# Linear attention and gated feed-forward, four layers: PSUM as four two-bank pairs, and attention scheduled by tiles

## The chip, the cores and the metric

The kernel runs on one core of a Trainium2 chip. The kernel before has a median of 1495.12 us.

TensorE is written PE (its weight loads PEld), VectorE DVE, ScalarE ACT, GpSimd POOL and SyncE SP, as in the profile.

## The reference, cut to what matters

```python
def _A_ref(x, wqkv, wo):               # x: 2048 x 1024, 32 heads of 32
    q, k, v = ...                       # x @ wqkv, by heads
    phi = lambda t: jnp.where(t > 0, t + 1, jnp.exp(t)) + 1e-6
    pq, pk = phi(q), phi(k)
    kv  = jnp.einsum("bhsd,bhse->bhde", pk, v)
    z   = jnp.einsum("bhsd->bhd", pk)
    num = jnp.einsum("bhqd,bhde->bhqe", pq, kv)
    den = jnp.einsum("bhqd,bhd->bhq", pq, z)[..., None] + 1e-6
    return (num / den) ... @ wo

def _B_ref(x, w_gate, w_up, w_down):    # hidden width 3584
    return ((x @ w_gate) * (x @ w_up)) @ w_down

x = A_x
x = x + _A_ref(_layernorm(x), A_wqkv, A_wo)
x = x + _B_ref(_layernorm(x), B_w_gate, B_w_up, B_w_down)
x = x + _A_ref(_layernorm(x), A_wqkv, A_wo)
x = x + _B_ref(_layernorm(x), B_w_gate, B_w_up, B_w_down)
```

The kernel calls the first and third lines "layer A" (attention) and the other two "layer B" (feed-forward). The same weights serve both layers of a kind. In a feed-forward layer the kernel forms seven products of half blocks, numbered 1 to 7, with sums in between, in place of eight; they run in the order 1, 2, 6, 5, 7, 3, 4.

## The kernel before: the parts that matter

PSUM is eight tiles of one bank each (128 x 512 float32). A "drain" below is an instruction of ACT or DVE that reads such a bank. `mm_tile` hands the banks out in turn.

```python
Q = [psum.tile([P, NB], F32, tag=f"Q{i}", name=f"Q{i}")[:] for i in range(8)]   # NB = 512

def phi(ps, dst, split=False):              # 512 columns
    e = turn("e", eb)
    # ... the split form takes a second ACT read (Identity) in place of DVE's read of PSUM
    nc.scalar.activation(out=e, in_=ps, func=ACT.Exp)
    nc.vector.tensor_scalar(out=e, in0=e, scalar1=1.0, scalar2=1e-6, op0=ALU.min, op1=ALU.add)
    nc.vector.scalar_tensor_tensor(out=dst, in0=ps, scalar=1.0 + 1e-6, in1=e, op0=ALU.add, op1=ALU.max)

def flush():                                # one pending action of a division
    if later:
        later.pop(0)()

def over_den(t):                            # division of one query tile: two actions
    # ...
    return [lambda: den_sums(pq, den), lambda: den_divide(t, pq, den)]
    # den_divide ends with the DMA transpose of the tile
```

While layer A runs for the first time, ACT also scans the weights of the feed-forward layers: a sum of squares of each of 42 blocks of 128 x 2048 (14 of gate, 14 of up, 14 of down). A scan needs its block in a buffer, and the end of a scan starts the fetch of a further block. The partial sums give a power-of-two scale per matrix: `scale_sum` on DVE, then one small matmul and a power in `scale_pow`.

```python
def scan_step(n=1):
    for _ in range(n):
        i = scanned[0]
        m, c = divmod(i, NU)                # NU = 14
        nc.scalar.activation(out=scan_buf[i], in_=scan_buf[i], func=ACT.Square, accum_out=acc[:, m, c:c + 1])
        scanned[0] += 1
        # ...
        scan_fetch()                        # DMA of a further block, issued from ACT's queue

def scale_sum(lo, hi):
    nc.vector.tensor_reduce(out=part[:, lo:hi], in_=acc[:, lo:hi, :], axis=AX.X, op=ALU.add)
    nc.vector.tensor_copy(out=partb[:, lo:hi], in_=part[:, lo:hi])

def scale_pow(lo, hi):
    ps = mm_tile()
    nc.tensor.matmul(out=ps[:, lo:hi], lhsT=ones[:], rhs=partb[:, lo:hi], start=True, stop=True)
    # ... max, power on POOL, bit mask
```

Layer A after the keys: query tiles, then kvo (the masked key-value product times the output weights), then output tiles, which also carry the last scans and the down scale:

```python
for t in range(XT_):                        # XT_ = 10
    q[2 * t]()
    scans()
    do(rest[...])                           # products xk, one bank each
    # ... t == 7: scale_sum(0, 2); t == 8: scale_pow(0, 2)
    q[2 * t + 1]()
    if t < 8:
        scans()
# ...
if first_A:
    # scale_sum(2, 3) in job 10, scale_pow(2, 3) in job 15
    for i in range(2, 9):                   # seven scans among the output tiles
        jobs[i] = [scans] + jobs.get(i, [])
```

Feed-forward: after products 1, 6 and 7 ACT copies the accumulator (a "snapshot"), as two copies of 512 columns; `vsum` on DVE adds two such halves to it later. The order of a unit, with the preparation of the next weights (`pr`) and of the down weights (`mine`, 2 us on ACT each, first layer only):

```python
elif p in (6, 7):
    snaps[u, p] = turn("sn", SN)
    for m in range(2):
        nc.scalar.copy(out=snaps[u, p][:, m, :], in_=a[m])
# ...
for u in range(NU):
    # ...
    gate_step(u, 1); gate_step(u - 1, 4)
    do(pr[0:2])
    gate_step(u, 2)
    pr[2]()
    gate_step(u - 1, 3); gate_step(u, 6)
    for x in mine: x[1]()                   # the down-weight scaling on ACT
    pr[3]()
    gate_step(u, 5); gate_step(u, 7)
    # ...
```

## Time and profile before

| | before |
|---|---|
| median of 3 runs | 1495.12 us (1494.37 to 1495.13) |
| span and granted clock of the profiled run | 1493.1 us, 1.00 |
| PE, DVE, ACT busy | 1477.1 (99%), 1060.9 (71%), 734.7 us (49%) |
| 364 matmuls of 512 columns in a row | 78.56 us, 215.8 ns each |

From the first part of the page of the kernel before, busy time of each engine in us, its share of the span, and the count of instructions:

```profile
PE 1477.1 (99%) x6895; PEld 675.9 (45%) x6997; DVE 1060.9 (71%) x1829; ACT 734.7 (49%) x914; POOL 66.4 (4%) x179
```

PE is the bound: 99% of the span at full clock. What can be won is the time in which PE starts no matmul. I read that in two ways: the view of waits, and the distances between starts of successive matmuls, in excess of 216 ns. The waits of PE in the kernel before (what PE waited for by line of the instruction and of its releaser: total, times, longest):

```profile
PE Q L528 <- ACT W L550: 1.1, 1, 1.1
...
PE Q L341 <- DMA XT<-ST: 0.9, 1, 0.9
PE Q L356 <- DVE K L331: 0.7, 1, 0.7
```

They are a few events of about 1 us each. L528 (products of the feed-forward layers) waits for a snapshot once; L341 (projections) for a DMA transpose once; L356 (xk) for phi once. In distances of starts these are 1.23, 1.10 and 0.88 us. (A missing record shows as a distance of twice 216 ns, and such distances are not counted as waits.)

The groups of instructions that the change widens, by shape (after the count: busy us, mean ns of one, then idle before and its releasers):

```profile
L218 ACT ACTIVATE K<-K 128x2048 bf16<-128x2048 bf16 x37 | 70.6, 1909 | 1.3 <-ACT K L218 0.9 <-DMA K<-in_B_w_down_dram 0.4
L550 ACT COPY MX<-Q 128x512 f32<-128x512 f32 x120 | 69.2, 585 | 96.4 <-PE Q L528 96.4
```

```profile
L493 DVE TENSOR_TENSOR W<-MX,Q 128x512 f16<-128x512 f32 x176 | 116.6, 684 | 28.7 <-ACT MX L550 16.5 <-PE Q L528 9.7
```

One snapshot of 512 columns takes ACT 585 ns, one sum DVE 684 ns. A scan takes 1909 ns, and 37 scans of this form waited for their fetch 0.4 us in all.

The scan starting at 208.81 is the last one; it ends at 210.7. Its partial sum is needed by the matmul of `scale_pow`, L233 in the timeline of PE:

```profile
214.63 0.16 PE L233 MATMUL Q<-partb,ones 128*128 128x1 bf16 x1
```

There is nothing in brackets: this matmul came 3.9 us after the end of the last scan, and PE did not wait. DVE's sum and copy take about 0.5 us of these, so the scan could have ended about 3.4 us later without a wait of PE. It is a margin of the scan alone.

### The profile page before, as it was taken

What the parts mean: (1) busy time and instruction counts of PE and PEld (TensorE: products, weight loads), DVE (VectorE), ACT (ScalarE), POOL (GpSimd) and SP (SyncE); (2) the same over time, 40 slices, a digit from 0 to 9 for tenths busy, and PEclk for the clock granted to TensorE, in tenths of its full rate; (3) what the DMA queues carried; (4) which work ended last, traced back from release to release, by engine and by line L of the source; (5) the groups of instructions that cost most, each with busy time, mean ns of one, the idle gap of its engine ahead of it and who ended that gap; (6) DMA issues with size and microseconds to landing.
All of it is one profiled execution on the core that took longest, in us unless ns stands there. A gap on an engine that the chain in (4) does not pass through costs nothing.

```text
span 1493.1 us, 18319 instructions
## 1 busy us (share of the span) xinstructions
PE 1477.1 (99%) x6895; PEld 675.9 (45%) x6997; DVE 1060.9 (71%) x1829; ACT 734.7 (49%) x914; POOL 66.4 (4%) x179
## 2 busy tenths in 40 slices
PE   8999999999999999999999999999999999999999
PEld 3444444444444444444444444444444444444444
DVE  7768878888775577768388567677776846777633
ACT  4988686777601466630023436556663016666200
POOL 3100011000000000001010000200000100000000
PEclk9999999999999999999999999999999999999999
DMA  7967947677555333327460115333332763333442
GB/s 216 250 191 178 237 127 204 197 217 211 193 166 171 83 93 94 92 100 225 134 170 0 22 36 120 85 85 96 95 87 99 233 173 95 85 85 85 153 167 83
DMA packets 277048, 202.79 MB, mean 136 GB/s; under 512 B 101984, under 2 KB 264288, under 8 KB 273376
## 3 DMA queue, kind: packets, MB, share of 16 engines
q1 hardware_dynamic: 261456, 182.61, 43.5%
q10 hardware_dynamic: 15504, 19.01, 4.1%
q8 instruction: 55, 0.90, 0.3%
q14 instruction: 33, 0.27, 0.1%
HBM read 160.43 MB, written 17.04 MB: 119 GB/s over the span
## 4 chain that ended last, share of the span: by engine, by line
PE 86%; ACT 1%; issue 0%; DVE 0%; ACTq 0%
PE Q L528 45%; PE Q L831 23%; PE Q L341 7%; PE Q L460 7%; PE Q L356 4%; ACT K L449 0%; PE Q L440 0%; ACT W L324 0%; PE Q L448 0%; PE Q L382 0%; ACT W L325 0%; ACT W L550 0%; DVE X L838 0%; PE Q L392 0%; ACTq L324 0%
## 5 line engine op out<-in xcount | busy, mean ns | idle before, releaser
L528 PEld LDWEIGHTS <-K 128*128 128x128 f16 x3136 | 306.9, 98 | 371.2 <-issue 1.3
L528 PE MATMUL Q<-XT,K 128*128 128x512 bf16 (+1 forms) x1734 | 398.7, 379 | 3.1
L831 PE MATMUL Q<-K,K 128*128 128x512 f16 (+2 forms) x1582 | 340.4, 377 | 0.0
L528 PE MATMUL Q<-TX,K 128*128 128x512 f16 x1344 | 308.3, 379 | 1.1 <-ACT W L550 1.1
L490 ACT ACTIVATE K<-K,fac 128x2048 f16<-128x2048 bf16 x112 | 218.4, 1998 | 127.5 <-PE Q L831 65.5
L831 PEld LDWEIGHTS <-K 128*128 128x128 f16 x1582 | 154.3, 98 | 184.5
L493 DVE TENSOR_TENSOR K<-K 128x1024 f16<-128x1024 f16 (+1 forms) x244 | 157.3, 666 | 37.1 <-ACT K L490 35.1
L493 DVE TENSOR_TENSOR W<-MX,Q 128x512 f16<-128x512 f32 x176 | 116.6, 684 | 28.7 <-ACT MX L550 16.5
L329 ACT ACTIVATE W<-Q 128x512 bf16<-128x512 f32 x90 | 52.8, 596 | 137.8 <-PE Q L341 127.0
L550 ACT COPY MX<-Q 128x512 f32<-128x512 f32 x120 | 69.2, 585 | 96.4 <-PE Q L528 96.4
L341 PE MATMUL Q<-K,XT 128*128 128x512 bf16 x500 | 113.9, 379 | 2.3 <-DMA XT<-ST 0.9
L341 PE MATMUL Q<-K,K 128*128 128x512 bf16 x497 | 113.8, 379 | 1.4 <-ACT K L449 0.7
L493 DVE TENSOR_TENSOR W<-W,Q 128x512 f16<-128x512 f32 x160 | 105.5, 684 | 11.5 <-ACT W L550 5.4
L550 ACT COPY W<-Q 128x512 f32<-128x512 f32 x104 | 60.3, 585 | 73.3 <-PE Q L528 73.3
L493 DVE TENSOR_TENSOR K<-K,K 128x512 f16<-128x512 f16 (+1 forms) x148 | 87.7, 597 | 4.2
L493 DVE TENSOR_TENSOR K<-W,Q 128x512 f16<-128x512 f16 x56 | 38.5, 687 | 73.0 <-PE Q L528 73.0
L838 DVE SCALAR_TENSOR_TENSOR W<-Q,kap,X 128x512 f32<-128x512 f32 x32 | 24.0, 750 | 77.6 <-PE Q L831 77.6
L341 PEld LDWEIGHTS <-K 128*128 128x128 bf16 x512 | 50.0, 98 | 61.0 <-issue 1.5
L341 PEld LDWEIGHTS <-XT 128*128 128x128 bf16 x512 | 49.4, 98 | 61.4 <-ACT XT L317 1.4
L532 DVE TENSOR_TENSOR K<-W 128x512 f16<-128x512 f16 x168 | 71.4, 425 | 5.8
L218 ACT ACTIVATE K<-K 128x2048 bf16<-128x2048 bf16 x37 | 70.6, 1909 | 1.3 <-ACT K L218 0.9
L252 DVE BATCH_NORM_STATS2 st<-X 128x6 f32<-128x512 bf16 x104 | 66.0, 675 | 3.1 <-DMA X<-in_A_x_dram 3.1
(116 smaller groups left out, 1180.9 us busy)
## 6 DMA issues: line engine op xcount, KB each, us to landing
K<-WD SPq DMA_DIRECT2D x28, 1792.0 KB, 7.4
K<-in_B_w_gate_dram SPq DMA_DIRECT2D x70, 512.0 KB, 4.0
K<-in_B_w_up_dram SPq DMA_DIRECT2D x56, 512.0 KB, 5.0
K<-in_A_wqkv_dram SPq DMA_DIRECT2D x10, 1024.0 KB, 7.7
K<-in_B_w_up_dram ACTq DMA_DIRECT2D x12, 512.0 KB, 4.0
K<-in_B_w_down_dram ACTq DMA_DIRECT2D x11, 512.0 KB, 4.0
K<-in_B_w_down_dram SPq DMA_DIRECT2D x10, 512.0 KB, 5.3
WD<-K SPq DMA_DIRECT2D x10, 512.0 KB, 3.0
```

The lines of the kernel that those rows point to most:

```text
L218: nc.scalar.activation(out=scan_buf[i], in_=scan_buf[i], func=ACT.Square, accum_out=acc[:, m, c:c + 1])
L252: nc.vector.bn_stats(out=stat[t][0][:, c, :], in_=X[:, t, c * NB:(c + 1) * NB])
L329: nc.scalar.activation(out=e, in_=ps, func=ACT.Exp)
L341: nc.tensor.matmul(out=ps, lhsT=xt[:, k, tl * P:(tl + 1) * P], rhs=w[:, k, :], start=(k == 0), stop=(k == KD - 1))
L356: nc.tensor.matmul(out=ps, lhsT=xn_a[t][:, j * P:(j + 1) * P], rhs=pk[t][:, n * NB:(n + 1) * NB], start=(t == 0), stop=(t == NT - 1))
L460: nc.tensor.matmul(out=ps, lhsT=xT[t // TPG][:, c, tl * P:(tl + 1) * P].bitcast(F16), rhs=KVo[n][:, c, :], start=(c == 0), stop=(c == KD - 1))
L490: nc.scalar.activation(out=b.bitcast(F16), in_=b, func=ACT.Copy, scale=fac[:, m:m + 1])
L493: eng.tensor_tensor(out=o, in0=a, in1=b, op=op)
L528: nc.tensor.matmul(out=pair[m], lhsT=stationary(n, p, m, k), rhs=moving[p][:, k, :], start=(p in (1, 2, 5) and k == 0), stop=(k == KH - 1) ...
L532: nc.vector.tensor_tensor(out=hA[i][:, u, :], in0=gu[:, 0, :], in1=gu[:, 1, :], op=ALU.mult)
L550: nc.scalar.copy(out=snaps[u, p][:, m, :], in_=a[m])
L831: nc.tensor.matmul(out=ps_[:, lo:hi], lhsT=act[:, u, j * P:(j + 1) * P], rhs=w[:, u, lo:hi], start=(p in (1, 2, 5) and u == 0), stop=(u == ...
```

## The change

Its intent: drain two banks with one instruction. One instruction on 1024 columns should be cheaper for ACT and DVE than two on 512. PSUM becomes one tile of eight banks, seen as eight banks or four pairs; phi, xk, the residual adds, the snapshots and the down sums work on pairs. The attention layers then go by tiles (query tile, two pairs of kvo, output tile), and a number of jobs move: scans, divisions, loads. The core of the diff:

```diff
-    Q = [psum.tile([P, NB], F32, tag=f"Q{i}", name=f"Q{i}")[:] for i in range(8)]
+    QQ = psum.tile([P, 8, NB], F32, tag="Q", name="Q")
+    Q = [QQ[:, i, :] for i in range(8)]
+    QP = [QQ[:, 2 * i:2 * i + 2, :] for i in range(4)]
 ...
     def load_o():
         for n in range(2):
-            nc.scalar.dma_start(out=wo[n], in_=wo_v[:, :, n * NB:(n + 1) * NB])
+            nc.sync.dma_start(out=wo[n], in_=wo_v[:, :, n * NB:(n + 1) * NB])
 ...
-    EARLY, MID = 32, 36
+    EARLY, MID = 26, 33
 ...
-        return [lambda: den_sums(pq, den), lambda: den_divide(t, pq, den)]
+        if t % 2 == 0:
+            ...
+            return [lambda: den_sums(t, pq, den)]
+        den, pq_ = dens.pop(t - 1)
+        return [lambda: den_sums(t, pq, den), lambda: den_divide(t - 1, pq_, den[:, 0, :]),
+                lambda: den_divide(t, pq, den[:, 1, :])]
 ...
-            for m in range(2):
-                nc.scalar.copy(out=snaps[u, p][:, m, :], in_=a[m])
+            nc.scalar.copy(out=snaps[u, p], in_=a)
 ...  layer A, query tiles
-        XT_ = 10
+        XT_ = 11
         for t in range(XT_):
 ...
+            scans(0 if t > 8 else 2 - t % 2)
 ...  layer A, jobs among the output tiles
-            for i, f in ((10, lambda: scale_sum(2, 3)), (9, dp[0][0]), (15, lambda: scale_pow(2, 3)), (13, dp[1][0])):
-                jobs[i] = jobs.get(i, []) + [f]
-            for i in range(2, 9):
-                jobs[i] = [scans] + jobs.get(i, [])
+            job(13, lambda: scale_sum(2, 3))
+            job(17, lambda: scale_pow(2, 3))
+            for i in range(2, 11):
+                job(i, scans)
 ...
+            out_tile(t)
+            if t < 3:
+                flush()
+                flush()
 ...  layer B, order of a unit
-                do(pr[0:2])
+                pr[0]()
                 gate_step(u, 2)
-                pr[2]()
                 gate_step(u - 1, 3)
                 gate_step(u, 6)
-                for x in mine:
-                    x[1]()
-                pr[3]()
+                pr[1]()
                 gate_step(u, 5)
+                pr[2]()
                 gate_step(u, 7)
+                pr[3]()
                 for x in mine:
+                    x[1]()
                     x[2]()
```

## The prediction

> **What bounds it now.** TensorE. The page has PE busy 1477 of 1493 us at clock 1.00. In the timeline of PE, 364 matmuls of 512 columns take 78.56 us, 215.8 ns each, back to back. The Trainium skill ("TensorE: Matmul & The Clock Gate", section "Wait — 56ns, not 53.3ns?") gives N/2.4 GHz + 2.5 ns = 215.7 ns at N = 512: the trace agrees, so this rate cannot improve. Both programs have the same number of PE instructions (order of instructions). About 6,792 full matmuls x 215.8 ns = 1465.7 us, 128-column work 10, start before the first transpose 6.9, tail after the last matmul 3.3: about 1486 us (estimate). Only some 7 us can be won.
>
> **Where these 7 us are** (starts of successive matmuls; waits of PE): 0.8 before the first projection; 1.1 at 34.0 us (transpose DMA of tile 7, issued behind four X loads); 0.9 at 69.5 (xk waits for the last phi); 0.9 at 180 to 187 (kvo copies, X add); 1.2 at 288.7 (snapshot behind the down-weight scaling on ACT, which waited 3.0 us for its DMA); 1.7 at 910 to 923 (kvo copies, split phi of the second attention layer). The feed-forward stages otherwise run without a gap.
>
> **What the change does.**
> - Two 512-column drains become one of 1024. This saves little: two ACT snapshots back to back take 1.05 us, one ACT copy of 1024 columns 1.01 to 1.05; two DVE sums 1.28 against about 1.23. And a drain starts only when both banks are done, 0.86 us later. DVE (71%) and ACT (49%) are off the path: gain about 0; I expect each 10 to 35 us less busy.
> - xk leaves the last two tiles to the end of each pair: the 0.9 at 69.5 goes.
> - The down-weight scaling moves behind product 7, so its DMA has more time: the 1.2 at 288.7 goes (it leaves about 2.5 us to spare, estimate).
> - kvo: four tiles with two pair kvo each: ACT 4.3 us (exp, identity, two scaled copies, about 1.05 to 1.1 each) against PE 4.32 per tile: just balanced. kvo 0 shares its pair with q tile 11 and waits for its identity: about 0.6 new, in each attention layer. Net gain 0.3 in the first, 1.0 in the second.
> - Start: half-width layernorm and transposes start the first projection 0.3 to 0.4 earlier, but statistics of tile 2 now stand behind the apply of tile 1: its transpose comes 0.7 later. Net 0 to 0.4 worse; the wait at tile 7 stays, about 1.
> - Scans are spread more evenly: no effect on PE.
>
> Sum: -0.9 - 1.2 - 1.3 + 0.3, and +0.5 for unforeseen waits: about -3 us.
>
> **Prediction: 1491.5 us**, 8 in 10 between 1487.5 and 1496.0. Faster by over 2%: 0.01; within 2%: 0.96; slower by over 2%: 0.03.
>
> **What shows it.** PE waits: none of xk on phi, none of feed-forward products on snapshots; one of 0.6 us at kvo 0, twice; the transpose wait at tile 7 still there. Spacing 215.8 ns unchanged. ACT and DVE with fewer instructions (595 and 1258 rows in the order against 828 and 1677), but little less busy.
>
> **What would make it wrong.** Output-weight loads now stand on SP behind semaphores of scan fetches: landing late, they stall kvo a few us. Down-weight scaling now blocks snapshot 1: a late DMA then costs up to once per unit. ACT over 4.3 us per tile in kvo adds up over four tiles. A better start gives 1 us more.

## More of the kernel before

The metric is the device time of one execution in microseconds (us).

The end of the scans in the kernel before, timeline of ACT (start in us, duration, instruction; in brackets the idle time before it and its releaser):

```profile
208.81 1.91 ACT L218 ACTIVATE K<-K 128x2048 bf16<-128x2048 bf16 x1 [0.41 <-DMA K<-in_B_w_down_dram]
210.63 0.19 ACT L218 ACTIVATION_READ_ACCUMULATOR K<-K 128x1 f32 x1
```

DVE reached the sum only in its turn, as its timeline shows:

```profile
214.23 0.15 DVE L227 TENSOR_REDUCE part<-acc 128x1 f32<-128x14 f32 x1
214.42 0.16 DVE L228 CAST partb<-part 128x1 bf16<-128x1 f32 x1
```

The copy ended at 214.58, 0.05 us before the matmul: on DVE's side there was next to no margin.

## The result, and the profile after

The changed kernel takes 1499.14 us (median of six fast runs, 1497.67 to 1501.46), the kernel before 1495.12 us beside it. The ratio is 1.0027, with a 95% interval of 1.0014 to 1.0040. (A ratio here is the mean time of one kernel's fast runs over the mean of the other's fast runs of the same rounds, so not quite the ratio of the medians quoted.) The change is within 2%, as expected, but it lost about 4 us where 3 to 4 us of gain were predicted, and the measured time lies outside the predicted range.

The same line of the changed kernel:

```profile
PE 1478.4 (99%) x6895; PEld 676.3 (45%) x6997; DVE 1007.7 (67%) x1426; ACT 709.6 (47%) x650; POOL 68.3 (5%) x178
```

DVE lost 53 us of busy time and ACT 25 us; PE has the same number of records. The span grew by 4.4 us. The waits of PE:

```profile
PE Q L236 <- DVE partb L231: 3.6, 1, 3.6
...
PE Q L372 <- DMA XT<-ST: 0.9, 1, 0.9
PE Q L372 <- DVE W L364: 0.8, 1, 0.8
PE Q L510 <- DVE X L512: 0.8, 2, 0.4
...
PE Q L500 <- ACT W L359: 0.4, 1, 0.4
...
PE Q L500 <- DMA TX<-in_A_wo_dram: 0.3, 1, 0.3
```

The wait of the feed-forward products for a snapshot is gone, and xk's wait for phi is down to 0.2 us. One wait of 3.6 us has come: L236, the matmul of `scale_pow`, waits for `partb`, the partial sums. The widened groups:

```profile
L221 ACT ACTIVATE K<-K 128x2048 bf16<-128x2048 bf16 x37 | 70.6, 1907 | 9.9 <-DMA K<-in_B_w_down_dram 5.7 <-ACT K L221 2.7 <-issue 1.0
...
L596 ACT COPY MX<-Q 128x1024 f32<-128x1024 f32 x60 | 60.8, 1013 | 122.4 <-PE Q L576 110.1 <-ACT K L538 12.3
```

```profile
L541 DVE TENSOR_TENSOR W<-MX,Q 128x1024 f16<-128x1024 f32 x88 | 107.4, 1221 | 38.4 <-PE Q L576 19.5 <-ACT MX L596 15.4
```

A snapshot of 1024 columns takes ACT 1013 ns, against 2 x 585 when counted singly; a sum takes DVE 1221 ns against 2 x 684. And the scans now waited for their fetches 5.7 us in all, against 0.4. The timelines of PE and DVE around the scale of the down weights:

```profile
215.82 3.62 PE L510 MATMUL Q<-K,K 128*128 128x512 bf16 x16
223.00 0.16 PE L236 MATMUL Q<-partb,ones 128*128 128x1 bf16 x1 [3.57 <-DVE partb L231]
```

```profile
222.59 0.17 DVE L230 TENSOR_REDUCE part<-acc 128x1 f32<-128x14 f32 x1 [8.02 <-ACT K L221]
```

DVE had stood idle for 8.02 us until the last scan (L221) ended. PE stood idle for 3.57 us before 223.00 (3.73 in distances of starts). What followed is in the table by stretches (busy time of each engine with the count of instructions, granted clock, share and rate of DMA):

```profile
223.00:226.40 3.40, 3.40 (x10) 1.19 (x10) 2.27 (x3) 3.40 (x7) 1.51 (x6) 0.50 0.29 110
226.40:230.00 3.60, 3.55 (x17) 1.68 (x17) 1.22 (x1) 3.60 (x6) 1.47 (x5) 1.00 0.38 73
```

For 3.4 us after the idle stretch the granted clock was 0.50. The trace has it at half from 223.02 to 226.43, 3.413 us, in which matmuls started 427 ns apart, seven such distances with a shorter one at each end. That cost another 1.66 us (0.16, 7 x 0.211 and 0.02). The Trainium skill ("TensorE: Matmul & The Clock Gate", section "What's actually happening") gives a window of 3413 ns by which the array's activity is judged, half clock after an idle window and full clock again after a busy one; the length of the dip agrees. The clock records of the other traces agree too (e11's has none): each switch within the work lies a whole number of 3.413 us after the first rise to full clock in its trace. Cut on this grid, stretches at full clock in which PE was idle for up to 1.95 us (kernel before, 4.72 to 8.13 us) were followed by full clock, and those with 2.14 us (e5) or more by half clock, with none in between.

Why were the sums late? The timeline of ACT before:

```profile
206.40 0.37 ACTq L213 DMA_DIRECT2D K<-in_B_w_down_dram  x1
207.75 1.91 ACT L221 ACTIVATE K<-K 128x2048 bf16<-128x2048 bf16 x1 [1.38 <-DMA K<-in_B_w_down_dram]
...
214.08 1.91 ACT L221 ACTIVATE K<-K 128x2048 bf16<-128x2048 bf16 x1 [4.33 <-DMA K<-in_B_w_down_dram]
...
220.57 1.89 ACT L221 ACTIVATE K<-K 128x2048 bf16<-128x2048 bf16 x1
```

A fetch issued at 206.40 landed at 214.05: 7.7 us, where a fetch of 512 KB took 3.6 to 4.1 us before and in the calm stretches. ACT waited 4.33 us for it. (The wait of 1.38 us was for the fetch issued at 203.95, which took 3.8 us as usual.) The norm of the next layer and the remaining scans stand behind in ACT's list and came after, from 216.59 on. The last scan ended at 222.46, against 210.7 before. The DMA issues of that time, the changed kernel from 202 to 215 us and the kernel before from 200 to 213 us (count, size, and median us to landing):

```profile
K<-in_B_w_down_dram ACTq DMA_DIRECT2D x3, 512.0 KB, 6.6
K<-MX SPq DMA_TRANSPOSE x2, 8.2
```

```profile
K<-in_B_w_down_dram ACTq DMA_DIRECT2D x2, 512.0 KB, 3.7
...
K<-MX SPq DMA_TRANSPOSE x1, 3.1
```

Two transposes were under way together (issued at 205.31 and 207.58), because two divisions are made at a time; each took 8.2 us in the median instead of 3.1, and the fetches beside them were slower too. Two transposes in flight are not enough for this: those issued at 196.13 and 198.40 overlapped as well, and took 4.0 and 3.2 us.

The account of the span, from starts of stages and from the distances of starts of matmuls:

| place | before, us lost | after, us lost |
|---|---|---|
| start, up to 16 us | 2.40 | 2.78 |
| transpose of tile 7 (34 us) | 1.10 | 1.03 |
| xk behind phi (70 to 73 us) | 0.88 | 0.38 |
| query tile 4 behind phi (102 us) | none | 0.95 |
| kvo and the start of the output tiles, first layer | 0.89 | 1.00 |
| output tile behind a residual add (212 us) | none | 0.54 |
| scale of the down weights (219 us) | none | 3.73 |
| half clock after it | none | 1.66 |
| snapshot in the feed-forward layer (289 us) | 1.23 | none |
| second attention layer | 1.65 | 0.55 |

Each row is read from one execution. The small rows before 100 us change from one to the next: the profiles of e1 to e4 below, whose code is the same up to there, show at most 0.20 us at tile 7 and 0.72 to 0.99 us at xk. The two large rows do not hang on this.

The first feed-forward layer starts 6.6 us later than before (248.9 against 242.3); the rows of the first layer, the half clock with them, give 6.8 more than before. The second feed-forward layer starts 4.2 us later (986.1 against 981.9): 2.4 us of the loss was won back, about the gain that the prediction had named for these two places (1.2 and 1.0). The end comes 4.4 us later.

### The profile page after: what moved, and what is told of

Same layout as the page of the kernel before. It is cut to its first block, busy times and chain, and to the rows that moved or that the text cites. A ratio compares the mean times of both kernels' runs of the same rounds, so it can differ in the third digit from the quotient of the medians.

```text
span 1497.5 us, 17477 instructions
## 1 busy us (share of the span) xinstructions
PE 1478.4 (99%) x6895; PEld 676.3 (45%) x6997; DVE 1007.7 (67%) x1426; ACT 709.6 (47%) x650; POOL 68.3 (5%) x178
## 5 line engine op out<-in xcount | busy, mean ns | idle before, releaser
L576 PE MATMUL Q<-XT,K 128*128 128x512 bf16 (+1 forms) x1734 | 394.5, 379 | 3.1
L538 ACT ACTIVATE K<-K,fac 128x2048 f16<-128x2048 bf16 x112 | 224.7, 2009 | 129.1 <-DMA K<-in_B_w_gate_dram 128.2
L355 ACT ACTIVATE W<-Q 128x1024 bf16<-128x1024 f32 (+1 forms) x68 | 65.8, 970 | 148.5 <-PE Q L372 143.6
L541 DVE TENSOR_TENSOR W<-MX,Q 128x1024 f16<-128x1024 f32 x88 | 107.4, 1221 | 38.4 <-PE Q L576 19.5
L596 ACT COPY MX<-Q 128x1024 f32<-128x1024 f32 x60 | 60.8, 1013 | 122.4 <-PE Q L576 110.1
L541 DVE TENSOR_TENSOR W<-W,Q 128x1024 f16<-128x1024 f32 x80 | 97.6, 1221 | 17.9 <-PE Q L576 13.2
L596 ACT COPY W<-Q 128x1024 f32<-128x1024 f32 x52 | 52.7, 1013 | 92.9 <-PE Q L576 79.9
L360 DVE TENSOR_SCALAR W<-W 128x1024 bf16<-128x1024 bf16 (+1 forms) x68 | 27.5, 404 | 83.5 <-ACT W L355 83.4
L221 ACT ACTIVATE K<-K 128x2048 bf16<-128x2048 bf16 x37 | 70.6, 1907 | 9.9 <-DMA K<-in_B_w_down_dram 5.7
L885 DVE SCALAR_TENSOR_TENSOR W<-Q,kap,X 128x1024 f32<-128x1024 f32 x16 | 20.5, 1284 | 65.8 <-PE Q L871 65.8
```

Source lines behind the costliest of these rows:

```text
L538: nc.scalar.activation(out=b.bitcast(F16), in_=b, func=ACT.Copy, scale=fac[:, m:m + 1])
L541: eng.tensor_tensor(out=o, in0=a, in1=b, op=op)
L576: nc.tensor.matmul(out=pair[:, m, :], lhsT=stationary(n, p, m, k), rhs=moving[p][:, k, :], start=(p in (1, 2, 5) and k == 0), stop=(k == K ...
L596: nc.scalar.copy(out=snaps[u, p], in_=a)
```

## The experiments

All fourteen kernels gave correct results, and each was timed against the kernel before in the same rounds. Unless it is said otherwise each edit is one of the changed kernel. First the table; the kernel before had medians of 1494.7 to 1496.0 us in these sessions.

| run | what it is | median us (range) | ratio to before | 95% interval |
|---|---|---|---|---|
| e1_scale_late | scale of down weights later | 1499.25 (1497.90 to 1501.10) | 1.0025 | 1.0011 to 1.0039 |
| e2_fill_wait | wait filled with matmuls | 1497.59 (1496.95 to 1498.59) | 1.0013 | 1.0001 to 1.0026 |
| e3_spaced | divisions one at a time | 1494.40 (1493.71 to 1494.99) | 0.9991 | 0.9978 to 1.0003 |
| e4_scans_early | two scans earlier | 1493.91 (1493.50 to 1496.53) | 0.9990 | 0.9978 to 1.0003 |
| e5_pairs_only | before, with pairs in layer B | 1504.09 (1502.96 to 1505.99) | 1.0059 | 1.0046 to 1.0071 |
| e6_order_only | before, with the new order in layer B | 1494.24 (1493.39 to 1494.47) | 0.9991 | 0.9977 to 1.0004 |
| e7_mended | scans and waits mended, first try | 1497.19 (1496.15 to 1498.66) | 1.0013 | 1.0001 to 1.0026 |
| e8_mended_start | e7 with another start | 1497.20 (1496.16 to 1498.67) | 1.0012 | 0.9999 to 1.0024 |
| e9_mended2 | second try | 1494.09 (1492.83 to 1496.48) | 1.0002 | 0.9989 to 1.0016 |
| e10_banks | e9 with single-bank drains in layer B | 1494.48 (1493.79 to 1496.81) | 1.0000 | 0.9987 to 1.0012 |
| e11_ffn_both | before, with pairs and order in layer B | 1494.27 (1494.16 to 1494.89) | 0.9997 | 0.9984 to 1.0011 |
| e12_mended3 | e9, sum and power later | 1497.83 (1495.19 to 1499.53) | 1.0020 | 1.0006 to 1.0034 |
| e13_pow_apart | e9, power alone later | 1492.59 (1492.21 to 1492.81) | 0.9983 | 0.9969 to 0.9997 |
| e14_both_remedies | e3 and e4 together | 1492.69 (1492.20 to 1493.01) | 0.9984 | 0.9971 to 0.9996 |

The first run of e11, the profiled one, took 3204.9 us; it is left out (see the last section).

### Moving the wait: e1_scale_late

```diff
-            job(13, lambda: scale_sum(2, 3))
+            job(18, lambda: scale_sum(2, 3))
-            job(17, lambda: scale_pow(2, 3))
-            job(19, lambda: scale_bits(2, 3))
+            job(20, lambda: scale_pow(2, 3))
+            job(22, lambda: scale_bits(2, 3))
-                job((20, 21, 26, 27)[i], f)
+                job((23, 24, 26, 27)[i], f)
```

> Edit of the changed kernel: the sum and the inverse root of the down weights' squares (with the one TensorE matmul in them) and the two first down preparations stand 2.5 and 1.5 output tiles later. Theory A (the 3.7 us wait of TensorE for the last scan at 219 us, and the 3.4 us at half clock that follow it, are what the change lost): both go, clock 1.000, time 1499.1 - 3.7 - 0.2 - 1.8 = about 1493.4 us. Rival B (ACT and DVE are late as a whole at the end of the first attention layer, and the wait only moves on): first products of the feed-forward stage wait instead, gain under 2 us, time over 1497.

Measured: 1499.25 us, no gain at all. The wait at 219 us was gone, but PE now waited elsewhere. Its waits in e1, and the stretch after the longest (PE alone; 0.53 is the granted clock):

```profile
PE Q L510 <- DVE X L512: 3.1, 3, 2.4
```

```profile
241.90:245.30 3.40, 3.24 (x8) 0.53 1.02 196
```

An output tile waited 2.4 us for a residual add (2.52 in distances of starts, at 239.3 us), and the half clock came after that wait instead. DVE stood in its list behind the results of the norm, and the norm stood behind the scans on ACT. In part the edit did this itself: the bit mask, moved as well, held DVE for 3.51 us at 234.62 until POOL's power was done, which stood behind steps of the norm. Further waits of 0.80 and 0.66 us came in the feed-forward layer. So the theory that the place of the small matmul is the cause, as I had put it, fell; its rival, that the wait moves on, held. The reading that fits is that ACT is late and each engine that needs it waits in turn; e1 alone does not show it, since the moved steps were in DVE's way.

### Filling the wait: e2_fill_wait

```diff
+        for _ in range(17 if lo == 2 else 0):
+            nc.tensor.matmul(out=ps, lhsT=ones[:], rhs=W[:, 5 * D:5 * D + NB], start=True, stop=True)
         nc.tensor.matmul(out=ps[:, lo:hi], lhsT=ones[:], rhs=partb[:, lo:hi], start=True, stop=True)
```

> Edit of the changed kernel: 17 useless matmuls of 512 columns (17 x 0.216 = 3.67 us) stand before the matmul that waits for the last scan, so the wait stays but TensorE is busy through it. Theory C (the half clock after 223 us comes from the idle TensorE): no matmul after it is at 427 ns, clock 1.000, and the time falls by the 8.5 x 0.211 = 1.8 us of the slow matmuls to about 1497.3 us, although work was added. Rival D (the clock drop has another cause): clock stays 0.998, time the same or up to 0.3 us longer, 1499.1 to 1499.5.

Measured: 1497.59 us against 1499.25 of e1, which shares its rounds; the granted clock of the profiled run is 1.000 and no distance of 427 ns is left. The seventeen matmuls, whose result is overwritten, occupy PE for as long as it waited before, so the lateness stays; what they win is the half clock, 1.66 us of the medians, as much as it had cost in the trace of the changed kernel. That the two agree to the digit is chance: the runs of e1 begin at 1497.90 us and those of e2 reach 1498.59. The clock is the firm part, 1.000 in all five runs. So the half clock comes from the idleness. The rest of the loss, the wait, is still in this run as useless work.

### Taking away the cause of the late fetch: e3_spaced

```diff
-            if t < 3:
-                flush()
-                flush()
+            if t < 6:
+                flush()
```

> Edit of the changed kernel: the pending divisions (each with its transpose DMA) are flushed one per output tile over six tiles instead of two per tile over three. Theory E (the scan's fetches land late, 7.7 us instead of 3.8, because two transposes fall on them at 205 to 214 us): the waits of ACT for the fetches (1.4 and 4.3 us) fall under 2 us in sum, the last scan ends about 4 us earlier, the wait at 219 us falls under 0.5 us and the half clock goes: about 1493.5 us. Rival F (the scans are late by their number: nine in the output tiles instead of seven): the wait at 219 us stays over 2.5 us, time 1498 or more.

The pending divisions, and with them the transposes, are made one per output tile instead of two. Measured: 1494.40 us, 4.9 us less than e1 in the same rounds. Fetches of that time took 3.5 to 4.2 us again. The timelines of ACT and of PE:

```profile
207.33 1.91 ACT L221 ACTIVATE K<-K 128x2048 bf16<-128x2048 bf16 x1 [1.06 <-DMA K<-in_B_w_down_dram]
...
209.97 1.91 ACT L221 ACTIVATE K<-K 128x2048 bf16<-128x2048 bf16 x1 [0.64 <-DMA K<-in_B_w_down_dram]
```

```profile
215.17 3.62 PE L510 MATMUL Q<-K,K 128*128 128x512 bf16 x16
218.96 0.16 PE L236 MATMUL Q<-partb,ones 128*128 128x1 bf16 x1 [0.18 <-DVE partb L231]
```

ACT waited 1.06 and 0.64 us for fetches in place of 1.38 and 4.33 (the transposes, 5.1 us each, still overlapped by 1.6 us), the last scan ended at 218.4, the small matmul waited 0.18 us (0.35 in distances), and the clock stayed at 1.00. The edit doesn't touch the scans or the place of the scale; so making the divisions, and with them the transposes, two at a time is one cause of the loss.

### Starting the scans earlier: e4_scans_early

```diff
-    EARLY, MID = 26, 33
+    EARLY, MID = 26, 35
-            scans(0 if t > 8 else 2 - t % 2)
+            scans(1 if t > 8 else 2 - t % 2)
-            for i in range(2, 11):
+            for i in range(2, 9):
                 job(i, scans)
```

> Edit of the changed kernel: two scans more before the kv step (35, as in the kernel before) and two fewer in the output tiles. Theory F (their number makes them late, each 2.5 us of ACT with its read and the issue of its next fetch): the last scan ends about 5 us earlier, the wait at 219 us goes, no half clock, about 1493.5 us. Theory E (the transposes' contention): the fetches still land late, the last scan ends at most 2 us earlier, a wait of 2 us or more stays, 1497 or more.

Seven scans among the output tiles, as in the kernel before, with the doubled transposes left in. Measured: 1493.91 us. The fetches were still slow (5.0 and 7.4 us; ACT waited 2.55 and 2.90 us), yet the last scan ended at 216.1, and the small matmul at 219.6 did not wait. The timelines of ACT and PE:

```profile
214.19 1.91 ACT L221 ACTIVATE K<-K 128x2048 bf16<-128x2048 bf16 x1 [2.90 <-DMA K<-in_B_w_down_dram]
```

```profile
219.62 0.17 PE L236 MATMUL Q<-partb,ones 128*128 128x1 bf16 x1
```

The two scans that moved delay phi of the last query tiles: the wait at kvo 0 grew from 0.55 to 1.06 us.

So neither the late fetch nor the late place of the scans is enough by itself: with either removed, the loss is gone but for a rest of 0.35 us in e3. In the prediction's terms, the two extra scans had used up the margin, and the slow fetch came on top: the last scan ended 11.7 us later than before, of which 7.7 us stay in e3, and the slow fetch makes about 4.1.

### The pairs alone, and the order alone: e5_pairs_only, e6_order_only, e11_ffn_both

These three are edits of the kernel before, in layer B only. e5 takes the pairs and keeps the old order of a unit:

```diff
-            for m in range(2):
-                nc.scalar.copy(out=snaps[u, p][:, m, :], in_=a[m])
+            nc.scalar.copy(out=snaps[u, p], in_=a)
 ...  and so for all sums and down sums of layer B
```

e6 takes the new order of a unit (the last part of the diff of the change) and keeps the banks; e11 takes both.

> The kernel before with only the two-bank pairs of the feed-forward layers put in (snapshots, sums and down sums on 1024 columns; attention layers and the order of the unit loop as before). Theory of the prediction (the drains are off the path): time within 1 us of the kernel before, ACT and DVE together 30 to 60 us less busy, the wait at 288.7 us still there or gone by chance. Rival (a drain that starts 0.86 us later delays products): waits of TensorE for snapshots, 3 us or more slower.

> The kernel before with only the changed order of the feed-forward unit loop (down-weight scaling behind product 7, preparations spread). Theory of the prediction: the wait for a snapshot at 288.7 us (1.2 us, and its kind) goes, 0 to 1.3 us faster than before. Rival (the scaling now blocks snapshot 1 and costs more): waits of products for snapshots of 1 us or more in several units, slower.

> The kernel before with both parts of the feed-forward change, pairs and unit order; its attention layers stay as before. The theory now: the pairs lose only under the old order (two 2 us conversions ahead of the snapshot of product 6), and the new order takes that away, so no product waits for a snapshot, clock 1.000, and the time is that of the order alone, 1493.5 to 1495. Rival (the pairs' loss is only covered in part): waits for snapshots of over 1 us in sum, 1496 or more.

Measured: e5 1504.09 us, 8.8 us over the kernel before by the ratio (0.0059 x 1495); e6 1494.24; e11 1494.27 over its four fast runs, each 1494.16 to 1494.89. The waits of e5:

```profile
PE Q L530 <- ACT MX L550: 4.0, 4, 2.2
PE Q L530 <- ACT W L550: 2.3, 2, 2.0
```

and the place of one of them, in the timelines of PE and ACT:

```profile
292.50 1.93 PE L530 MATMUL Q<-TX,K 128*128 128x512 f16 x7 [2.02 <-ACT W L550]
```

```profile
289.55 2.00 ACT L588 ACTIVATE K<-K,fac 128x2048 f16<-128x2048 bf16 x1 [3.15 <-DMA K<-in_B_w_down_dram]
291.46 0.99 ACT L550 COPY W<-Q 128x1024 f32<-128x1024 f32 x1
```

It is the wait that the kernel before has at the same place (1.23 us): the down-weight scaling waits for its DMA on ACT, and the snapshot of product 7 stands behind it. With single banks PE went on after the first half of the snapshot (copy from 289.51 on, 0.59 us; matmul at 290.13); with a pair it needs the whole copy, 0.99 us, and the distance came to 2.40 us, an excess of 2.18. Of the 0.95 us more than before, the copy explains 0.4; the rest is that the scaling itself began 0.5 us later against PE's work. There is one more like it at 379.1 us (2.41), a half clock after each, and at the start of each of the four passes 0.78 us, where two conversions of 2 us stand ahead of the snapshot of product 6. My expectation that pairs by themselves cost nothing was wrong, and so was the sentence of the prediction that says "gain about 0". The Trainium skill ("Perfetto Trace Analysis", section "Optimizing Scalar/DVE Operations") says that where ACT or DVE are not saturated but make other engines wait, breaking instructions up may let work complete sooner. ACT is at 47% in e5, and this agrees, from the other side: joining the copies under the old order cost 8.8 us. With the new order, which moves the scaling behind the snapshot of product 7 and spreads the preparations, there was no difference left to see: e11 against e6, 0.9997 and 0.9991 with overlapping intervals. (That no product waits for a snapshot is seen in the changed kernel; e11's only trace is of its slow run.)

The order alone did what was predicted of it: the wait at 289 us (1.23 us) is gone in e6's profile, and the ratio of 0.9991 is 1.3 us, though its interval includes 1.

### A mended version: e7 to e10

e7 takes the spaced divisions of e3, spreads the scans differently again, lets kvo 0 of the first layer have a free pair, and loads X later so that the transpose of tile 7 isn't behind it:

```diff
-    EARLY, MID = 26, 33
+    EARLY, MID = 26, 34
-            scans(0 if t > 8 else 2 - t % 2)
+            scans(2 if t < 9 else t == 9)
-            ps = turn("kvo", QP[2:4])
+            ps = turn("kvo", [QP[3], QP[2]] if c_first[0] else QP[2:4])
-                if i == 2:
+                if i == 4:
                     for x in range(3 * TPG, NT):
 ...  spaced divisions as in e3; other counts of scans among keys and xk
```

e8 is e7 with the statistics of tile 2 split around the layernorm of tile 1, as in the kernel before.

> The changed kernel with its waits mended: divisions flushed one per output tile; scans moved out of the last K tiles and the third xk pair into the q tiles, 34 before kv and 8 after; kvo 0 on the pair that q tile 11 does not use; the last X loads issued after tile 7's transpose. If the losses of the change are these waits and the half clock alone: no wait over 0.5 us between 34 and 220 us, clock 1.000, 8 to 10 us under the changed kernel, 1489 to 1491. If instead ACT or DVE has no room for the scans in the q tiles: new waits on phi there, time over 1493.

> As e7_mended, and the first half of tile 2's statistics stands ahead of the apply of tile 1 again, as in the kernel before. The prediction's reading of the start (tile 2's transpose comes 0.7 us late because its statistics stand behind that apply): the wait of TensorE for TX at 10.6 us falls from 0.8 to under 0.3 us and the time by about 0.5 us against e7_mended. Rival (the start is bound by the arrival of X): no change.

Measured: 1497.19 and 1497.20 us; both expectations failed. The waits at 102, 212 and 954 us were gone as intended, and that at 34 us, which is nearly gone in e1 to e4 without an edit; xk's, 1.06 us, stayed. But a new one had come, the longest of e7:

```profile
PE Q L502 <- DMA TX<-in_A_wo_dram: 2.6, 1, 2.6
```

The output weights, which the change loads from SP's queue, were issued at 163.81 and 164.40 us behind waits for other things, landed at 172.0 and 175.0, and PE waited 2.78 us (distance of starts) for them; a half clock followed. The prediction had named this as something that would make it wrong; in the changed kernel itself it showed with only 0.3 us, because there the loads went out at 160.7 and 161.3. e8's start lost 0.54 and 0.41 us where e7's lost 0.40 and 0.81, and the total did not move. e8's profile also shows what a second wait nearby does (PE alone, cut nearly on the grid of 3.413 us):

```profile
170.90:174.25 3.35, 1.28 (x6) 1.00 1.10 349
174.30:177.70 3.40, 2.36 (x6) 0.50 1.21 297
177.70:181.10 3.40, 3.40 (x9) 0.50 0.86 202
```

A wait of 0.73 us and most of one of 2.75 us fell into the first stretch, the rest of the second into the next, and half clock lasted for two stretches, 6.8 us.

e9 puts these loads back on ACT's queue and distributes the scans once more (fewer among the last keys, more among xk and the queries):

```diff
-            nc.sync.dma_start(out=wo[n], in_=wo_v[:, :, n * NB:(n + 1) * NB])
+            nc.scalar.dma_start(out=wo[n], in_=wo_v[:, :, n * NB:(n + 1) * NB])
-                if 10 <= i <= 28 and i % 2 == 0:
+                if 10 <= i <= 26 and i % 2 == 0:
-            scans(3)
+            scans(3 if i < 2 else 2)
-            scans(0 if t > 8 else 2 - t % 2)
+            scans(0 if t > 8 else 2 - (t % 4 == 3))
-                if t > 10 and n == 1:
+                if t > 13 and n == 1:
 ...  kvo pair, X loads and spaced divisions as in e7
```

e10 is e9 with the snapshots and sums of layer B as two halves each.

> The changed kernel with: one division flushed per output tile; output weights loaded from ACT's queue again, as before; kvo 0 on the free pair; X loads behind tile 7's transpose; one scan less at the end of the K tiles and one less behind the third xk pair, two more in the q tiles; the key sums of tiles 11 to 13 behind the K tiles. If the losses are those waits: no wait over 0.5 us after the start but at most one, the stage up to the first feed-forward product ends at 240 to 241.5 us (242.3 before, 248.9 changed), clock 1.000, 1488.5 to 1490.5 us. If the output weights are held by DMA traffic and not by SP's order: the wait at kvo stays at 0.4 us or more.

> As e9_mended2, but every drain of the feed-forward layers (snapshots, sums, down sums) is two instructions of 512 columns again, in the new order. If the wide drains are worth nothing to TensorE once the order is right: same time as e9_mended2 within 0.7 us, with ACT about 5 us and DVE about 10 to 20 us more busy. If the wide drains themselves buy time: e9_mended2 is over 1 us faster.

Measured, and the expectation of 1488.5 to 1490.5 us failed: e9 1494.09 us, in two groups: 1492.83, 1493.64, 1494.09, and 1496.23, 1496.48. e10 1494.48, with one run at 1496.81, which is the profiled one. In e10 ACT is 739.5 us busy and DVE 1029.3, against 710.1 and 1007.7 in e9, and the times do not differ within their scatter: the saved 29 us of ACT (5 had been expected) and 22 us of DVE win nothing that is seen here. The profile of e9 shows 1.0 us lost at 154 us, at the matmul of `scale_pow` for gate and up; the profile of e10 2.82 us at the same place and a half clock behind it. That made this wait the suspect for the two groups. The recorded clocks of e9's upper two runs are 0.999 (1496.48) and 1.000 (1496.23), so a half clock can explain at most one of them.

### The suspect of the two groups: e12_mended3, e13_pow_apart

e12 moves the sum, the power and the bit mask of the gate and up scale one attention tile later. e13 moves only the power and the bit mask and leaves the sum:

```diff
 e12, of e9
-            elif first_A and t == 7:
+            elif first_A and t == 8:
                 scale_sum(0, 2)
-            elif first_A and t == 8:
+            elif first_A and t == 9:
                 scale_pow(0, 2)
-            elif first_A and t == 9:
+            elif first_A and t == 10:
                 scale_bits(0, 2)
 e13, of e9: the same without the first pair of lines
```

> The edit of e9_mended2 with the sum, the power and the bit mask of the gate and up scale one attention tile later each. In e9 the power's matmul came at 154 us before the partial sums of the last gate/up scan and TensorE waited 1.0 us, 0.84 of it in that wait; in the two of five runs of e9 near 1496.4 and in the profiled run of e10 (2.82 us there) the wait was longer and brought a half clock. If this wait is what splits e9's runs in two, all runs of e12 have clock 1.000, no wait at the power of gate and up, and the times lie together at 1491.5 to 1494.0, ratio to the kernel before 0.9975 to 0.9995. If the two groups come from something else (the chip's own drift), runs near 1496 appear again and the ratio stays at 1.000. A new wait may appear in place of it: the bit mask and the masked products of kv now follow each other closely; under 0.5 us expected.

Measured: 1497.83 us, all runs from 1495.19 to 1499.53. The expectation failed completely. The wait had grown. The timelines of PE and DVE of e12:

```profile
162.40 0.16 PE L236 MATMUL Q<-partb,ones 128*128 128x2 bf16 x1 [3.83 <-DVE partb L231]
```

```profile
151.74 0.43 DVE L360 TENSOR_SCALAR W<-W 128x1024 bf16<-128x1024 bf16 x1 [5.86 <-ACT W L355]
...
161.96 0.17 DVE L230 TENSOR_REDUCE part<-acc 128x2 f32<-128x28 f32 x1
```

DVE had stood idle for 5.86 us behind an exponential of ACT, which stood behind scans that had waited 3.37 and 0.45 us for fetches; then it worked its list off, and in e12 that list had the rest of a further phi (from 156.38) and then the sums and the first division of a pair of tiles (158.03 to 162.05) ahead of the sum. By moving sum and power together I had kept their distance on PE and put more work of DVE ahead of the sum. In e9 the sum stood at 154.93 behind a shorter piece. So a wait for `partb` depends on what stands ahead of the sum in DVE's list, and not on the scans alone, and I could not yet say what splits the runs.

> The edit of e9_mended2 with the sum of the gate and up partials where it was and only the power's matmul and the bit mask one attention tile later, so about 4.3 us more of matmuls stand between sum and power. If the wait for the partials at the power is what splits the runs of e9 (1492.8 to 1494.1 and 1496.2 to 1496.5), no wait over 0.3 us at the power, clock 1.000 in all five runs, all of them between 1491.5 and 1494.5, ratio 0.9975 to 0.9995. If the split comes from elsewhere, runs above 1496 appear again although the power does not wait.

Measured: 1492.59 us, all five runs within 1492.21 and 1492.81, clock 1.000 in each, no wait at the power of gate and up. The timelines of DVE and PE:

```profile
155.75 0.17 DVE L231 CAST partb<-part 128x2 bf16<-128x2 f32 x1
```

```profile
158.12 0.17 PE L236 MATMUL Q<-partb,ones 128*128 128x2 bf16 x1
```

The sum came no earlier than in e9, where the copy began at 155.14, but PE now asked for it 2.2 us after the copy's end. This is what the theory of the wait had said. e9 and e13 differ in nothing but the place of the power and the mask, and the upper group is gone with five runs out of five; e9 had two of five there. That the wait is mended is shown; that it had split e9's runs is not. Five runs against five are few, the two ran in different rounds, and the clock of 1.000 at 1496.23 us does not fit. The kernel before ran from 1493.31 to 1497.54 in the same rounds.

### Both remedies and nothing else: e14_both_remedies

The edits of e3 and e4 together.

> The changed kernel with both remedies and nothing else: divisions spaced one action per tile over six tiles, and nine of the late scans moved before the output tiles. If the two remove the same loss (the wait at the down scale's power and the half clock after it), the time is that of either alone, 1493.5 to 1494.8, ratio 0.998 to 1.0; if they add up, about 1489 to 1490. Waits that stay: phi at 72 and 102 us, and kvo 0, which in the run with early scans had grown to 1.06 us.

(The expectation says nine scans; the edit moves two, as in e4.) Measured: 1492.69 us (1492.20 to 1493.01), ratio 0.9984 [0.9971, 0.9996]. It is below the range for "the same loss" by 0.8 us and far from the sum of the two. Mostly, then, the two remove one loss, with about 1 us more (by the ratios) from what e3 and e4 each had left: the waits at 212 and 954 us are gone, which were still in e4, and the wait of 0.35 us at the small matmul, which was still in e3. (That is read from distances in single profiles; the intervals of e3, e4 and e14 overlap.) The remaining losses in e14 are the start, 0.86 us at the transpose of tile 7, 0.47 at xk, 1.48 at query tile 4 and 0.63 at kvo 0.

e13 and e14 are faster than the kernel before by 0.17 and 0.16% with intervals just clear of 1, and faster than the changed kernel by about 6.5 us of their medians (not of the same rounds). By the measure of 2% all are the same.

## Why the prediction was wrong, point by point

- **The bound and the spacing held.** PE starts a matmul of 512 columns every 215.8 ns; the Trainium skill ("TensorE: Matmul & The Clock Gate", section "Wait — 56ns, not 53.3ns?") has 215.7. PE is 99% busy in both kernels. DVE and ACT lost busy time (53 and 25 us; 10 to 35 each had been expected, so DVE's was under-estimated), and e10 shows no time won by it.
- **The step that failed: "Scans are spread more evenly: no effect on PE."** They are not only spread: two more stand among the output tiles, and their fetches run beside doubled transposes. The last scan moved by 11.7 us (its end from 210.7 to 222.5), the place of the matmul that needs it by only 4.6 us (from 214.63 to where it would have started without a wait, 219.27), and the margin was 3.4 us: that leaves 3.7 us (11.7 less 4.6 less 3.4), and PE lost 3.73 us in the wait and 1.66 us in half clock. In the sum of the prediction this term stood at 0. e3 and e4 each remove it by touching one of its two causes, and e2 separates the half clock from the wait. Without these 5.4 us the changed kernel would have come in at about 1493.7 (1499.1 less 5.4, worked out), inside the range and about 2 us above the point.
- **The allowance for the unforeseen was too small: "+0.5 for unforeseen waits".** Besides the above, the profile has 0.95 us at query tile 4 (its exponential stands behind three scans on ACT, 2.45 to 3.01 us each with the read of the sum and the issue of fetches), and 0.54 and 0.55 us at output tiles that wait for residual adds, with DVE backed up by divisions made in pairs. That is 2.0 us, four times the allowance, and most of the rest of the error.
- **"Two 512-column drains become one of 1024 … gain about 0" held only together with the new order.** e5 shows +8.8 us for the pairs alone, e6 and e11 none for the two together. I had costed the busy time (1.05 us to 1.01 to 1.05) and had noted that a drain starts later, but not what stands ahead of it on ACT.
- **"The 1.2 at 288.7 goes" held**: no product waits for a snapshot in the changed kernel. **"The 0.9 at 69.5 goes"** did not hold: 0.38 us stayed in the profile of the changed kernel, 0.72 to 0.99 us in those of e1 to e4 with the same code up to there.
- **"About 0.6 new, in each attention layer" at kvo 0** came once: 0.55 us in the first layer and none in the second. A further 0.44 us came in the first, of which 0.3 us is the DMA of output weights. The net gain of this stage was −0.1 us in the first layer (predicted 0.3) and 1.1 us in the second with the residual add's 0.55 counted (predicted 1.0).
- **The start** lost 0.38 us more (predicted 0 to 0.4), and the wait at tile 7 stayed, 1.03 us (predicted about 1), in this profile; in those of e1 to e4 it is 0.20 us or less.
- **What stays open.** Why the kernel before scatters over 4 us while e13 and e14 scatter over 0.8 us in the same rounds was not tested. Half clock is not the reason: all nine of its runs there have a clock of 1.000. That two transposes in flight slow a fetch beside them is seen in the changed kernel and goes away in e3; the experiment changed their timing as a whole, so what in the DMA engines is contended was not shown.

## What to carry to other kernels

When a bound engine waits for a small result at a fixed place in its list, write down the margin between the end of the chain and that place before you move anything of the chain; the work that is "off the path" has just that margin, and here it was about 3.4 us. In these runs more than about 2 us of idle TensorE within one stretch of the 3.413 us grid cost twice, once as the wait and once as a stretch at half clock. A long wait split into several short ones is a gain only if they fall into different stretches: in e8 two waits in one stretch added up. Wider drains save busy time on an engine that may not need it, and they make whatever stands ahead of them cost more: widen only together with an order in which nothing long stands ahead of a drain that is due.

## What the Trainium skill lacked or had wrong

- "TensorE: Matmul & The Clock Gate", section "Back-to-back issue gap", gives about 131 ns per matmul as the sustained rate at 512 columns in a stream of weight loads and matmuls, and calls the formula with 216 ns too high for this. In this kernel's stream of that kind, 364 matmuls in a row took 215.8 ns each: the formula is right here and the sustained figure is not reached.
- The same page, section "What's actually happening", has the half clock after at least one idle window of about 3.4 us. Here waits of 2.18 us (e5), 2.41 (e5), 2.52 (e1) and 2.78 us (e7) already brought it, in the distances of starts, and 3.73 us in the changed kernel. Distances of 1.0 to 1.7 us (e2, e4, e14) did not: the clock stayed at 1.00. What counted in these traces is the idle time within one stretch of the 3.413 us grid: up to 1.95 us kept full clock and 2.14 us or more brought half clock. So a window need not be wholly idle, and the wait of 3.99 us in e12, cut by the grid into 1.45 and 2.57 us, brought half clock only after the second part.
- No page that I found gives what the read of an accumulated sum costs ACT, or a scan in all: 0.19 us to read the accumulator, and with 0.37 us to issue the next fetch from the same queue 2.44 us from one scan of 128 x 2048 to the next in a row (changed kernel, 201.93 to 204.37; the scan itself is 1.9 us).
- No page that I found tells by how much DMA transposes and plain loads that are in flight together slow each other: two overlapping transposes of one tile took 8.2 us in the median instead of 3.1, and a load of 512 KB beside them 7.7 us instead of 3.6 to 4.1; another two, 9 us earlier, overlapped and took 4.0 and 3.2 us.
- No page that I found explains a run like the profiled one of e11: 3204.9 us instead of 1494, with matmuls of 512 columns 443 ns apart in the median and a fifth of them about 559, in the first of five runs of one program. Its trace holds no record of the clock, so the 1.0 listed for it says nothing. It is not explained here either.
